# A retention and gated-MLP kernel: five reorderings, of block 1's scaling, of GpSimd's sums, of stores and transposes in SP's queue, and of the last tile's results

## The chip, the cores and the metric

The kernel runs on one core of a Trainium2 chip. A core has five engines with instruction streams of their own: TensorE (PE, matrix products into PSUM), VectorE (DVE), ScalarE (ACT), GpSimd (POOL) and SyncE (SP, which here only issues DMAs). They meet through semaphores. The metric is the device time of one execution in microseconds; lower is better. PSUM has eight banks; the kernel's tags `n` and `st` hold one bank each, `a`, `b` and `m` two each.

## The reference

Retention attention for 8 batches, 8 heads, 576 positions and head size 64, and behind it a layer of 512 to 2048 to 512 with the activation h cos(h), without a bias or a softmax:

```python
def _attn_ref(q, k, v):
    scale = 1.0 / np.sqrt(D_)
    scores = scale * np.matmul(q, k.transpose(0, 1, 3, 2))
    gamma = 1.0 - 2.0 ** (-5.0 - np.arange(H))
    rel = pos[:, None] - pos[None, :]
    Dmat = np.where(rel >= 0, gamma[:, None, None] ** rel[None, :, :], 0.0)
    return np.matmul(scores * Dmat, v)

def _moe_ref(x, w_in, w_out):          # x: 4608 x 512
    h = x @ w_in                       # 512 x 2048
    g = h * np.cos(h)
    return g @ w_out                   # 2048 x 512
```

Inputs and the output are float32.

## The kernel before

The 4608 tokens are cut into 18 **blocks** of 256 (`j`) and into 9 **tiles** of 512 (`n`, two blocks each).

*Retention.* gamma to the power of a difference is a product of a factor of the row and one of the column, so q and k are scaled by tables of powers (`scaled`, L167), rounded to bf16, transposed, and multiplied (`scores`); a mask leaves the causal half (`ret`, L262, L292). Within 128 tokens the sum over v is direct (`out_own`, L375); everything earlier comes through a running state (`sums_of`, L319, with the adds at L338 to L349), whose rounded copy multiplies q (`out_carried`, L407). The sum of both is copied as `xT`.

*Transposes.* Blocks 0 to 3 are transposed on TensorE (`transpose_pe`, L210, with a copy at L215). Blocks 4 to 17 are transposed by DMA (`transpose_dma`, L197), 14 in all, issued on SP. `step` prepares one block: q and k scaled on GpSimd (`prep`), the DMA transpose, v rounded on GpSimd, and then the loads of a later block (`load`, five to eight DMAs on SP). So GpSimd's and SP's queues hold the blocks in the order in which the program calls `step`, together with the stores of results (`stored_rows`, L579). Below, "transpose 8" is that of block 8.

*The layer.* `mm1` makes h in PSUM for four or two rows of 128 of the 2048, ScalarE takes the cosine (as a sine of h plus pi/2, L457) and VectorE multiplies (L460) into `gT`. The second product of tile 0 is direct (L927). From tile 1 on it is done as seven products instead of eight on 2x2 blocks (`mm2_seven`, `product`, L563), with sums of quarters of `gT` (`g_sum`, L503, called `gs`) and of the weights (`w_sums`, L483) ahead of them. Product x has the numbers 1 to 7; the order is 1, 2, 4, 6, 5, 7, 3 in tile 1 and 1, 2, 6, 4, 7, 5, 3 later. Results are copied from PSUM by ScalarE (`copied`, L593), added up by VectorE (L589), and stored as four quarters c11, c21, c22 and u1 (store numbers 0, 1, 2 and 3). Adds and stores are put on a list `pend` and run at the next `flush`. After a store of a given number, `stored` may call `steps_to`, which prepares blocks up to a number.

*Sums on GpSimd.* VectorE makes most of the `gs`; GpSimd makes that of product 3 in tile 1 and that of product 7 later, in pieces of 128x512. In tile 1 the work of `first_scores` lies between products 4 and 6: the second halves of gs 5 and gs 6, the mask products of block 4, gs 3, gs 7 and the state sums of block 5.

*The last tile.* Its product 5 is computed in three pieces, one of 256 columns and two of 128, and product 3 is accumulated on the same pieces, so that the last adds and stores are small. In `product` the first piece has the tag `b`; the two small ones share a tile with the tag `m`. Stores alternate between SP and ScalarE for c22 and for the last three pieces.

The order of the instructions on each engine is that of the program: the schedule is written by hand, and only waits on semaphores are put in by the framework. It tracks them by tile: a reader of a tile waits for its last writer. `after` adds a wait by hand, for which `g_sum` has the argument `gate`.

Of the kernel before, what the change touches and what calls it, by code (L numbers as in the profile page):

```python
# [8 lines left out]
F32 = mybir.dt.float32  # L9
# [8 lines left out]
def kernel(  # L18
# [9 lines left out]
    nc = tc.nc  # L28
    P = 128
# [12 lines left out]
    E2 = ET // 2  # L42
# [489 lines left out]
    def product(n, x, halfway=None):  # L532
        gT = tiles["g", n]
        parts = [(j, 0, N2) for j in range(2)]
        fold = n in (1, last)
        fresh = x not in ((6, 7, 3) if fold else (6, 7))
        if fresh:
            tag = {1: "n", 2: "st", 4: "m" if n == 1 else "st", 5: "st", 3: "n"}[x]
            if x == 5 and n == last:
                ps = psum.tile([P, N2], F32, tag="b", name="o")  # L540
                pt = psum.tile([P, 2, 512], F32, tag="m", name="o")
                tiles["o", x] = [ps] + [pt[:, k, : N2 // 2] for k in range(2)]
            else:
                ps = psum.tile([P, 2, N2], F32, tag=tag, name="o")
                tiles["o", x] = [ps[:, j] for j in range(2)]
                tiles["all", x] = ps
        if x in (5, 3) and n == last:
            parts = [(0, 0, N2), (1, 0, N2 // 2), (1, N2 // 2, N2)]
        dst = tiles["o", x if fresh else 5 if x == 3 else 1]
        lhs = {1: gT[:, :E2, :256], 2: gT[:, E2:, :256], 4: gT[:, E2:, 256:]}.get(x)  # L550
        if lhs is None:
            lhs = tiles["gs", n, x]
        rhs = {1: w_quarter(0, 0), 2: w_quarter(1, 0), 3: w_quarter(1, 1)}.get(x)
        if rhs is None:
            rhs = w_sum[x]
        order = [(e, i) for e in range(E2) for i in range(len(parts))]
        if len(parts) > 2:
            order.sort(key=lambda u: u[1])
        for u, (e, i) in enumerate(order):
            if halfway and u == len(order) // 2:  # L560
                halfway()
            j, c0, c1 = parts[i]
            nc.tensor.matmul(  # L563
                dst[i],
                lhsT=lhs[:, e, j * P : (j + 1) * P],
                rhs=rhs[:, e, c0:c1],
                start=(fresh and e == 0 and (i == 0 or len(parts) > 2)),
                stop=(e == E2 - 1 and (i == len(parts) - 1 or len(parts) > 2)),
                skip_group_check=True,
            )  # L570
        return parts
# [9 lines left out]
    def mm2_seven(n, at, stored, xs=(1, 2, 6, 4, 7, 5, 3), halfway=None):  # L581
# [13 lines left out]

        def store(t, r, c, s):
            def go():
                queues = (nc.sync, nc.scalar) if n == last and s == 2 else (nc.sync, nc.sync)
                stored_rows(n * W + r * 256, c * N2, (c + 1) * N2, t, queues)
                stored(s)  # L600

            return go

        for x in xs:
            if x in at:
                at[x](flush, pend)
            else:
                flush()
            if x == 6 and n > 1:
                late_sums(n, (3,))  # L610
            parts = product(n, x, halfway)
            if x == 1:
                c11 = copied("a", 1)
                tiles["c11"] = c11
                if n > 1 and 2 not in at:
                    late_sums(n, (5, 6))
            elif x == 2:
                c11 = tiles["c11"]
                if n == 1:
                    p2 = copied("d", 2)  # L620
                    continue
                pend[:0] = [add(c11, c11, tiles["all", 2]), store(c11, 0, 0, 0)]
            elif x == 6:
                u1 = copied("b", 1)
            elif x == 4:
                c21 = copied("c", 4)
            elif x == 7 and n == 1:
                pend += [
                    add(c21, c21, tiles["all", 1]),
                    add(c22, c22, tiles["all", 1]),  # L630
                    store(c21, 1, 0, 1),
                    store(c22, 1, 1, 2),
                    add(c11, c11, p2),
                    store(c11, 0, 0, 0),
                ]
            elif x == 7:
                c22 = copied("d", 1)
                pend += [add(c21, c21, tiles["all", 1]), store(c21, 1, 0, 1)]
            elif x == 5 and n == 1:
                c22 = copied("d", 5)  # L640
            elif x == 5 and n == last:
                for (j, c0, c1), ps in zip(parts, tiles["o", 5]):
                    pend.append(add(c22[:, j, c0:c1], ps, c22[:, j, c0:c1]))
                pend.append(store(c22, 1, 1, 2))
            elif x == 5:
                pend += [
                    add(c22, c22, tiles["all", 5]),
                    add(u1, u1, tiles["all", 5]),
                    store(c22, 1, 1, 2),
                ]  # L650
            elif n < last:
                pend += [add(u1, u1, tiles["all", 5 if n == 1 else 3]), store(u1, 0, 1, 3)]
                flush()
            else:
                flush()
                for (j, c0, c1), ps in zip(parts, tiles["o", 5]):
                    add(u1[:, j, c0:c1], ps, u1[:, j, c0:c1])()
                    stored_rows(
                        n * W + j * P, N2 + c0, N2 + c1, u1[:, j : j + 1, c0:c1],
                        (nc.sync, nc.scalar),  # L660
                    )
# [124 lines left out]
    load_next(names="kqv", gate=w_dma[3])  # L786
    ps0 = psum.tile([P, DG, BK], F32, tag="m", name="ov")
    out_own(0, ps0)
    transpose_pe(1, "k", "st", vec, (1,))
    scaled(nc.vector, 1, "q", 0)  # L790
    scaled(nc.vector, 1, "q", 1)
    out_carried(0, ps0)
    act(x_of(0), ps0)
    nc.scalar.activation(sine, half_pi, ACTF.Sin, bias=0.0, scale=1.0)
# [70 lines left out]
    for n in range(NT):  # L865
        blocks = blocks_of.get(n) or [(e + k * E2, 0, W) for e in range(0, E2, 2) for k in range(2)]
        for i, (et, c0, cw) in enumerate(blocks):
# [11 lines left out]
            if (n, i) == (1, 0):  # L879
                step(False)  # L880
                load_next()
                for r0, ot in stores:
                    stored_rows(r0, 0, DM, ot)
            if (n, i) == (1, 1):
                step(False)
                load_next()
                step()
            if (n, i) == (1, 3):
# [75 lines left out]

        def first_scores(flush, pend):
            g_sum(n, 5, 4, E2)
            g_sum(n, 6, 4, E2)
            masks = scores(a, "ab")
            add_a = sums_of(a, "st")
            add_b = sums_of(b, "m")  # L970
            masks[0]()
            add_a()()
            masks[1]()
            g_sum(n, 3, 0, E2)
            g_sum(n, 7, 0, 4)
            tiles["rounded"] = add_b()
            g_sum(n, 7, 4, E2)

        def next_scores(flush, pend):
            outputs(a, "a")  # L980
# [30 lines left out]

        def stored(u):
            if n == 1:
                steps_to({2: 8}.get(u, 0))
            else:
                steps_to({0: 2 * n + 6, 3: 2 * n + 7}.get(u, 0))

# [31 lines left out]
```

## Time and profile before

| | before |
|---|---|
| median of 3 runs | 296.59 us (295.59 to 298.37) |
| the profiled execution | 296.28 us |
| its span, first to last instruction | 294.6 us |
| TensorE busy | 283.2 us (96%) |
| VectorE busy | 215.6 us (73%) |
| ScalarE, GpSimd busy | 143.0, 145.6 us (49% each) |
| mean granted TensorE clock | 0.994 |
| data moved by DMA | 49.78 MB |
| median from issue to landing: store of 128 KB, transpose | 2.6, 5.1 us |

Times in a view count from the start of the span. In the chain that ended last a row has its start, its length and what it is: an engine with the tile and the line, or a DMA from issue to landing. In the timeline a row has start, length, engine, line, operation, what is written from what, shapes and a count; rows of the same kind that follow each other are merged, and behind them stands how long the engine had been idle and what ended that. `SPq` and `ACTq` are the queues of SP and ScalarE in which DMAs are issued: the length there is that of the issue, not of the transfer. In the list of waits a row has who waited for whom, the total, how often, and the longest.

### The profile page before, as it was taken

The numbers are of one execution on the slowest core, as the hardware profiler recorded it, in microseconds if no ns is written. First come the engines' busy times: TensorE is split into PE (matmuls) and PEld (weight loads), VectorE is DVE, ScalarE is ACT, GpSimd is POOL, SyncE is SP. The second block draws the span as 40 slices with busy tenths as digits, with TensorE's granted clock in tenths as the row PEclk, the third lists the DMA queues.
The fourth block names the chain that finished last, engine by engine and source line by source line (L and its number), as shares of the span: only waits on it lengthen the run. The fifth ranks groups of instructions, "written<-read, shape, count | busy, mean of one in ns | idle before, by whom it ended". The sixth has DMA issues, their size and how long they took to land.

```text
span 294.6 us, 7623 instructions
## 1 busy us (share of the span) xinstructions
PE 283.2 (96%) x3248; PEld 195.0 (66%) x3268; DVE 215.6 (73%) x268; ACT 143.0 (49%) x166; POOL 145.6 (49%) x172
## 2 busy tenths in 40 slices
PE   7889999999999999999999999999999999999993
PEld 2568755878864688458845884588458845874583
DVE  4585748558986999699659965996599659835933
ACT  4466537646436624563356335633563356326620
POOL 8641535847864495839713961497148014102400
PEclk9799999999999999999999999999999999999999
DMA  7999999999899999999999999979930630121014
GB/s 197 268 222 215 232 247 214 231 181 231 198 199 227 204 240 210 191 219 197 236 203 193 243 215 197 219 128 223 203 64 21 127 71 0 38 65 44 2 37 107
DMA packets 128930, 49.78 MB, mean 169 GB/s; under 512 B 89344, under 2 KB 128384, under 8 KB 128896
## 3 DMA queue, kind: packets, MB, share of 16 engines
q1 hardware_dynamic: 124288, 44.84, 75.6%
q0 software_dynamic: 4224, 4.19, 8.8%
q8 instruction: 25, 0.41, 0.6%
q10 hardware_dynamic: 384, 0.26, 0.4%
q14 instruction: 9, 0.07, 0.1%
HBM read 36.70 MB, written 9.44 MB: 157 GB/s over the span
## 4 chain that ended last, share of the span: by engine, by line
PE 79%; DVE 10%; DMA 4%; POOL 2%; ACT 2%; issue 1%; DVEq 0%; ACTq 0%
PE h L445 38%; PE o L563 27%; PE o L927 5%; DVE gT L460 3%; PE ov L375 3%; DVE gs L503 3%; DMA qkT<-qks 2%; PE st L319 2%; POOL qks L167 2%; PE sc L282 2%; DVE ret L292 2%; PE ov L407 1%; DMA fk<-in_k_dram 1%; PE tr L210 1%; ACT cosh L457 1%
## 5 line engine op out<-in xcount | busy, mean ns | idle before, releaser
L445 PE MATMUL h<-xT,w_in_sb 128*128 128x512 bf16 (+1 forms) x690 | 126.6, 340 | 1.0
L460 DVE TENSOR_TENSOR gT<-h,cosh 128x1024 bf16<-128x1024 f32 x72 | 87.9, 1221 | 37.5 <-ACT cosh L457 37.4
L457 ACT ACTIVATE cosh<-h,half_pi 128x1024 f32<-128x1024 f32 x72 | 80.2, 1114 | 66.4 <-PE h L445 65.1
L445 PEld LDWEIGHTS <-w_in_sb 128*128 128x128 bf16 x704 | 68.4, 98 | 55.3 <-issue 0.6
L503 POOL TENSOR_TENSOR gs<-gT 128x512 bf16<-128x512 bf16 x28 | 35.8, 1280 | 92.2 <-DVE gT L460 92.2
L563 PEld LDWEIGHTS <-gs 128*128 128x128 bf16 x528 | 49.5, 98 | 6.4
L167 POOL TENSOR_TENSOR qks<-fq,gq 128x512 bf16<-128x512 f32 x31 | 33.9, 1113 | 18.1 <-DMA fq<-in_q_dram 14.9
L563 PEld LDWEIGHTS <-gT 128*128 128x128 bf16 x384 | 37.1, 98 | 6.3
L593 ACT COPY ot<-o 128x512 f32<-128x512 f32 x33 | 19.3, 586 | 40.5 <-PE o L563 40.5
L167 POOL TENSOR_TENSOR qks<-fk,gkc 128x512 bf16<-128x512 f32 x28 | 31.8, 1154 | 0.0
L589 DVE TENSOR_TENSOR ot<-ot,o 128x512 f32<-128x512 f32 x35 | 23.2, 680 | 10.9 <-ACT ot L593 7.9
L563 PE MATMUL o<-w_out_sb,gs 128*128 128x256 bf16 (+1 forms) x264 | 30.6, 269 | 0.0
L563 PE MATMUL o<-ws,gs 128*128 128x256 bf16 (+1 forms) x264 | 30.5, 270 | 0.0
L563 PE MATMUL o<-w_out_sb,gT 128*128 128x256 bf16 x256 | 30.5, 273 | 0.0
L292 DVE TENSOR_TENSOR ret<-sc,mask_c 128x1024 bf16<-128x1024 f32 x25 | 29.7, 1214 | 0.1
L430 ACT CAST xT<-ov 128x1024 bf16<-128x1024 f32 x16 | 16.2, 1013 | 11.0 <-PE ov L407 11.0
L178 POOL CAST vb<-fv 128x512 bf16<-128x512 f32 x31 | 18.7, 624 | 5.7 <-DMA fv<-in_v_dram 5.6
L503 DVE TENSOR_TENSOR gs<-gs,gT 128x1024 bf16<-128x1024 bf16 x16 | 15.7, 982 | 0.3
L503 DVE TENSOR_TENSOR gs<-gT 128x512 bf16<-128x512 bf16 (+1 forms) x25 | 15.4, 615 | 0.4
L563 PE MATMUL o<-ws,gT 128*128 128x256 bf16 x128 | 15.3, 273 | 0.0
L349 DVE TENSOR_TENSOR s<-st,s 128x256 f32<-128x256 f32 x18 | 7.6, 421 | 10.4 <-PE st L319 10.1
L359 ACT CAST sb<-s 128x512 bf16<-128x512 f32 (+1 forms) x18 | 10.3, 573 | 9.3 <-DVE s L347 3.8
(81 smaller groups left out, 203.4 us busy)
## 6 DMA issues: line engine op xcount, KB each, us to landing
out_dram<-ot SPq DMA_DIRECT2D x69, 128.0 KB, 2.6
fk<-in_k_dram SPq DMA_DIRECT2D x25, 256.0 KB, 5.7
fv<-in_v_dram SPq DMA_DIRECT2D x25, 256.0 KB, 5.1
fq<-in_q_dram SPq DMA_DIRECT2D x12, 512.0 KB, 5.3
w_in_sb<-in_moe_w_in_dram POOLq DMA_DIRECT2D x4, 512.0 KB, 8.1
w_out_sb<-in_moe_w_out_dram POOLq DMA_DIRECT2D x4, 512.0 KB, 9.8
fk<-in_k_dram SPq DMA_DIRECT2D x3, 512.0 KB, 5.3
fv<-in_v_dram SPq DMA_DIRECT2D x3, 512.0 KB, 7.0
```

The source lines that it names most:

```text
L167: return eng.tensor_tensor(out=dst.rearrange("p b a d -> p a b d"), in0=src.rearrange("p (a b) d -> p a b d", a=2), in1=by.rearrange("p (a ...
L178: runs[y](vb[:, y], f[:, :, y, :] if j < NP_B else f[:, y])
L292: nc.vector.tensor_tensor(out=ret[:, k].rearrange("p a b i -> p (a b) i"), in0=pss[k].rearrange("p a b i -> p (a b) i"), in1=mask.unsqueez ...
L430: evac(x, ps)
L445: nc.tensor.matmul(ps[:, j, :], lhsT=w_in_sb[:, dg, (et + j) * P : (et + j + 1) * P], rhs=xT[:, dg, c0 : c0 + w], start=(dg == 0), stop=(d ...
L457: nc.scalar.activation(cosh, ps, ACTF.Sin, bias=half_pi, scale=1.0)
L460: nc.vector.tensor_mul(gT[:, et : et + m, c0 : c0 + w], ps, cosh)
L503: i = eng.tensor_tensor(out=tiles["gs", n, x][:, e : e + step], in0=a[:, e : e + step], in1=b[:, e : e + step], op=op_,)
L563: nc.tensor.matmul(dst[i], lhsT=lhs[:, e, j * P : (j + 1) * P], rhs=rhs[:, e, c0:c1], start=(fresh and e == 0 and (i == 0 or len(parts) > 2)),
L589: return lambda: nc.vector.tensor_tensor(out=out_, in0=in0, in1=in1, op=ALU.add)
L593: nc.scalar.copy(t, tiles["all", x])
L927: nc.tensor.matmul(pss[t], lhsT=gT[:, e, t * P : (t + 1) * P], rhs=w_out_sb[:, e, :], start=(e == 0), stop=(e == ET - 1),)
```

## The change

- Block 1's two scalings of q on VectorE stand ahead of the transpose and copy of the second half of its k.
- The stores of tile 0 stand behind the preparation of block 5 and no longer ahead of it, the fourth row first. The steps that tile 1's third store (c22) set off are set off by its fourth (u1).
- In tile 1, GpSimd's sum for product 3 is cut in two halves. The first waits for VectorE's second half of gs 6, the other for its second half of gs 7.
- In the last tile, the add and store of c21 are called at once behind product 7 and ahead of the copy of c22; of the store of c21 one half is issued on ScalarE, as that of c22 was already.
- In the last tile, the two small pieces of products 5 and 3 have a PSUM tile of their own each, with the tags `m` and `a`.

No instruction is added or taken away on an engine; one DMA moves from SP's queue to ScalarE's.

```diff
--- before.py
+++ after.py
@@ -537,9 +537,10 @@
         if fresh:
             tag = {1: "n", 2: "st", 4: "m" if n == 1 else "st", 5: "st", 3: "n"}[x]
             if x == 5 and n == last:
-                ps = psum.tile([P, N2], F32, tag="b", name="o")
-                pt = psum.tile([P, 2, 512], F32, tag="m", name="o")
-                tiles["o", x] = [ps] + [pt[:, k, : N2 // 2] for k in range(2)]
+                tiles["o", x] = [
+                    psum.tile([P, c], F32, tag=t, name="o")
+                    for t, c in (("b", N2), ("m", N2 // 2), ("a", N2 // 2))
+                ]
             else:
                 ps = psum.tile([P, 2, N2], F32, tag=tag, name="o")
                 tiles["o", x] = [ps[:, j] for j in range(2)]
@@ -595,7 +596,7 @@
 
         def store(t, r, c, s):
             def go():
-                queues = (nc.sync, nc.scalar) if n == last and s == 2 else (nc.sync, nc.sync)
+                queues = (nc.sync, nc.scalar) if n == last and s else (nc.sync, nc.sync)
                 stored_rows(n * W + r * 256, c * N2, (c + 1) * N2, t, queues)
                 stored(s)
 
@@ -634,8 +635,10 @@
                     store(c11, 0, 0, 0),
                 ]
             elif x == 7:
+                pend += [add(c21, c21, tiles["all", 1]), store(c21, 1, 0, 1)]
+                if n == last:
+                    flush()
                 c22 = copied("d", 1)
-                pend += [add(c21, c21, tiles["all", 1]), store(c21, 1, 0, 1)]
             elif x == 5 and n == 1:
                 c22 = copied("d", 5)
             elif x == 5 and n == last:
@@ -786,9 +789,9 @@
     load_next(names="kqv", gate=w_dma[3])
     ps0 = psum.tile([P, DG, BK], F32, tag="m", name="ov")
     out_own(0, ps0)
-    transpose_pe(1, "k", "st", vec, (1,))
     scaled(nc.vector, 1, "q", 0)
     scaled(nc.vector, 1, "q", 1)
+    transpose_pe(1, "k", "st", vec, (1,))
     out_carried(0, ps0)
     act(x_of(0), ps0)
     nc.scalar.activation(sine, half_pi, ACTF.Sin, bias=0.0, scale=1.0)
@@ -879,10 +882,10 @@
             if (n, i) == (1, 0):
                 step(False)
                 load_next()
-                for r0, ot in stores:
-                    stored_rows(r0, 0, DM, ot)
             if (n, i) == (1, 1):
                 step(False)
+                for r0, ot in stores[3:] + stores[:3]:
+                    stored_rows(r0, 0, DM, ot)
                 load_next()
                 step()
             if (n, i) == (1, 3):
@@ -964,17 +967,18 @@
 
         def first_scores(flush, pend):
             g_sum(n, 5, 4, E2)
-            g_sum(n, 6, 4, E2)
+            six = g_sum(n, 6, 4, E2)
             masks = scores(a, "ab")
             add_a = sums_of(a, "st")
             add_b = sums_of(b, "m")
             masks[0]()
             add_a()()
             masks[1]()
-            g_sum(n, 3, 0, E2)
+            g_sum(n, 3, 0, 4, gate=six)
             g_sum(n, 7, 0, 4)
             tiles["rounded"] = add_b()
-            g_sum(n, 7, 4, E2)
+            seven = g_sum(n, 7, 4, E2)
+            g_sum(n, 3, 4, E2, gate=seven)
 
         def next_scores(flush, pend):
             outputs(a, "a")
@@ -1011,7 +1015,7 @@
 
         def stored(u):
             if n == 1:
-                steps_to({2: 8}.get(u, 0))
+                steps_to({3: 8}.get(u, 0))
             else:
                 steps_to({0: 2 * n + 6, 3: 2 * n + 7}.get(u, 0))
 
```

## The prediction

> **What bounds the kernel now.** I read the chain that ended last first, in order of time, because the change touches five separate places and only the chain says which of them sets the end.
>
> ```profile
> PE 79%; DVE 10%; DMA 4%; POOL 2%; ACT 2%; issue 1%; DVEq 0%; ACTq 0%
> ```
>
> ```profile
> 14.49 0.43 DVE qkT L215
> 14.91 1.21 DVE qks L167 x2
> ...
> 108.92 6.22 DMA qkT<-qks
> 115.14 0.04 issue
> 115.19 0.64 PE sc L282 x32
> ...
> 277.65 12.41 PE o L563 x128
> 290.08 0.29 DVE ot L589
> ```
>
> TensorE is busy 283.2 of 294.6 us. Before 18 us the chain runs through VectorE; at 115.19 us scores wait for a DMA transpose; after that it is TensorE without a break up to the last product. So a gain ahead of 115 us counts only if that transpose lets it through, and every wait added behind it counts in full. Next the waits of TensorE: all that exceeds 0.3 us, once the start is left out, is small.
>
> ```profile
> PE tr L210 <- DVE qks L167: 2.2, 6, 0.7
> PE sc L282 <- DVE s L349: 0.4, 1, 0.4
> PE ov L375 <- DVE ret L292: 0.2, 1, 0.2
> PE sc L282 <- DMA qkT<-qks: 0.2, 1, 0.2
> ```
>
> **Part 1, block 1's q scaled ahead of the copy.** In the timeline of VectorE the copy at 14.49 us waits 1.37 us for transposes, while q's scaling (14.83, 1.28 us for two) needs only q of block 1, which landed at 12.2 (issued 4.97, 7.3 to landing). After the change scaling runs at 13.12 to 14.41 and hides in that wait; the copy of k stays at 14.49. TensorE's transposes of q, now at 15.57 and 16.17, can follow its two idle matmuls at 15.0, so the two copies run at 15.45 and 15.87 and end at 16.3 instead of 17.02. Scores of block 1 start at 16.35, not 17.08: **-0.75 us**. Cover behind it: the next matmuls need weights that landed at 14.5, 19.9 and 22.4 us (issue plus 7.2, 7.2, 9.0); the tightest, at about 23.4 now and 22.65 then, keeps 0.3 us.
>
> **Part 2, GpSimd's sums in halves.** The timeline of VectorE in the second tile's products:
>
> ```profile
> 75.16 1.53 DVE L503 TENSOR_TENSOR gs<-gs,gT 128x1024 bf16<-128x1024 bf16 x1
> 76.61 2.34 DVE L292 TENSOR_TENSOR ret<-sc,mask_c 128x1024 bf16<-128x1024 f32 x2
> 78.88 1.60 DVE L503 TENSOR_TENSOR gs<-gT 128x1024 bf16<-128x1024 bf16 x1
> 80.40 0.87 DVE L349 TENSOR_TENSOR s<-st,s 128x256 f32<-128x256 f32 x2
> 81.19 0.68 DVE L503 TENSOR_TENSOR gs<-gT 128x1024 bf16<-128x1024 bf16 x1
> ```
>
> The same 128x1024 sum takes 0.68 us alone and 1.53 and 1.60 us while GpSimd's four sums run (74.50 to 79.94). The gates put GpSimd's first two behind the first of these and its last two behind the last, so VectorE saves 0.85 + 0.92 = 1.77 us. GpSimd's first half then takes two of its undisturbed 1.15 us and ends about when the second sum begins; its last half runs some 80.5 to 82.8, ahead of product 3 at 84.9 and of its own next work at 83.83, which waits for a load. So nothing queued behind the gated sums is late. TensorE gets back its two waits here, 0.38 us for s and 0.25 us for ret: **-0.63 us**. The Trainium skill (SBUF — State Buffer, Who interferes with whom) says that the second to start fully blocks until the first is done; the 1.60 us row agrees, since GpSimd's last sum ended at 79.93 and 0.68 more gives 80.6 against 80.48. By that rule a GpSimd half that ran late would cost one sum up to 1.15 us again, which changes nothing in the total below.
>
> **Part 3, order on SP's queue.** Two moves. Transpose 5 goes ahead of the first tile's eight stores: it is issued at about 68.9 us instead of 74.88, and its scores come at 80.55 where it now lands at 79.4, so it leaves the way free for the earlier TensorE. The eight stores move some 3 us back; the first reuse of their buffers waits for the store that is put first. The other move is that all eight stores of the second tile go ahead of transpose 7, four of them formerly behind the loads of block 9:
>
> ```profile
> 93.85 3.14 SPq L579 DMA_DIRECT2D out_dram<-ot  x4
> 97.59 2.27 SPq L197 DMA_TRANSPOSE qkT<-qks  x1
> 99.90 0.72 SPq L135 DMA_DIRECT2D fq<-in_q_dram  x1
> ...
> 105.25 3.56 SPq L579 DMA_DIRECT2D out_dram<-ot  x4
> 108.92 3.10 SPq L197 DMA_TRANSPOSE qkT<-qks  x1
> ```
>
> SP issues back to back from 38 to 130 us, so its order is the order of landing, and TensorE's pace doesn't reach it. Transpose 7 is issued 3.1 to 3.6 us later, lands at 104 to 106, and is needed at 111: free. Transpose 8, the one TensorE waits for, has the same work ahead of it: 97.03 + 3.14 to 3.56 for four stores + 7.66 (from transpose 7 to the end of five loads) = 107.8 to 108.3, up to 1.2 more if transpose 5 behind loads holds SP 3.3 to 3.6 us like its likes instead of 2.27. GpSimd has its input by 107.4 now, earlier then. But it stands right behind loads now. The two that stand so take 6.9 and 6.7 us to landing (issues 58.20, 84.42); the shortest of any takes 4.4, this one 6.2. That gives 112.2 at best, 114.5 to 116.4 with the likes of it; I take **115.3**. TensorE, 1.38 us earlier, would be there at 113.6 (114.97 less 1.38). It waits, and starts at 115.35 instead of 115.19: parts 1 to 3 together **+0.15 us**; between -1.6 (no wait at all: 1.38 and the present 0.22) and +3.1 (below).
>
> **Part 4, the last tile.** The end is a chain of four engines:
>
> ```profile
> 286.42 0.59 ACT L593 COPY ot<-o 128x512 f32<-128x512 f32 x1 [1.16 <-PE o L563]
> ```
>
> ```profile
> 287.04 0.69 DVE L589 TENSOR_TENSOR ot<-ot,o 128x512 f32<-128x512 f32 x1 [4.51 <-ACT ot L593]
> 287.65 1.03 DVE L589 TENSOR_TENSOR ot<-o,ot 128x256 f32<-128x256 f32 x3
> ```
>
> ```profile
> 288.76 0.73 ACTq L579 DMA_DIRECT2D out_dram<-ot  x1
> ```
>
> ScalarE copies c22, VectorE adds c21, then the three pieces of c22; product 3 at 288.12 follows the first piece's add. The change turns it round: the add of c21 starts at 286.42 and ends at 287.11; ScalarE's queue then holds a store that waits for this add, and only behind it the copy. An issue on ScalarE took 0.47 to 0.73 us, so the copy runs from about 287.85 to 288.45 instead of ending at 287.01. Queued behind the copy: VectorE's first c22 piece (288.45 instead of 287.65), behind that product 3 on TensorE, which waits for it, and the final adds. **+0.80 us**. Own results for the pieces let the add of the middle piece start 0.4 us sooner, and moving a store off SP frees 0.60 us of SP; but SP's last three stores (289.79, 290.58, 291.22) follow each other at issue pace from the first piece's add (ends 289.61), which is itself 0.8 later. They gain 0.1 at most: SP was free at 289.70. The Trainium skill (DMA: Bandwidth & Descriptors, Issuing engines are not separate DMA queues) says that a second issuing engine saves only issue time, usually small beside the transfer; 0.60 against 2.4 us to landing agrees. By that the move to ScalarE buys at most its 0.60 on SP, nothing in landing.
>
> **Sum.** The profiled execution took 296.28 us (span 294.6), 0.31 under the median of 296.59. 296.28 + 0.15 + 0.80 = **297.2 us**, 0.2% over the median. A measurement of this kernel tells about 1% (3 us) from no change.
>
> **Rivals.**
> *Transpose 8 lands early.* With stores filling the gaps that transposes leave, loads come sooner and it lands by 113.6. For: 4.4 us is the shortest latency. Against: both transposes behind loads took 6.7 or more. 296.28 - 1.6 + 0.8 = 295.5.
> *Slower: the late transpose 7 is not made good.* In the rows eight stores keep SP for 6.7 us while each needs about 0.35 us of transfer (so far apart land those queued behind loads); if the DMA engines stand idle meanwhile, transpose 7 and the loads behind it slip by 3.1 us, and transpose 8 with them, to 118.2: 296.28 + 3.1 + 0.8 = 300.2. It passes 1% once 2.2 of the 3.1 are lost. Against: four stores fewer behind the loads give 3.56 back.
> *ScalarE is not held by its issue.* Then the copy starts at 287.2, and the tail costs 0.15: 296.6.
> *The gates do not part the two engines* (rows of 1.5 us stay): -0.63 goes, but transpose 8 decides all the same: 297.2.
>
> **Chances.** Forecast (the last rival in it) 0.50, early transpose 0.20, cheap tail 0.15, slower 0.11; 0.04 for a gain of over 1%, for which the profile has no source: removable waits add to 1.6 us. Runs of one kernel scatter (up to 298.37 before), which puts 0.01 of the forecast over the bound: faster 0.04, same 0.84, slower 0.12. The range leaves out the far half of the slow rival and the quickest of the early one: 295.3 to 299.3.
>
> **What would show it.** Right: scores of block 1 at 16.4; gs sums of 0.7 us near 75 and 78; TensorE waiting 1 to 2 us for a transpose near 114; ScalarE's copy of c22 ending near or after 2 us behind product 7, and product 3 waiting 0.8 us for VectorE. Wrong: no wait near 114 (then the DMA order gained), or a wait of over 3 us there; a last copy as soon as now.

## The result, and the profile after

The changed kernel took **299.84 us** (median of six runs, 299.56 to 302.02), the kernel before 296.22 in the same measurement (295.59 to 298.37). The ratio is 1.0127, with a 95% interval of 1.0082 to 1.0171. The prediction of 297.2 us, in a range of 295.3 to 299.3, was too low: the change makes the kernel slower by 1.3%, and not by 0.2%.

The profiled execution of the changed kernel took 299.81 us, with a span of 298.1 us against 294.6 before. The views of this section are of this pair. In the changed file the lines behind the edited store function stand one further down, so that L563, L579, L589 and L593 of before are L564, L580, L590 and L594 here.

The first view is the chain that ended last, in order of time (start, length, what). This is the piece of it that answers to the transpose at 108.92 us and the scores at 115.19 before:

```profile
109.82 6.32 DMA qkT<-qks
116.14 0.04 issue
116.18 1.01 PE sc L282 x32
117.20 3.09 PE o L564 x16
```

Transpose 8 is issued 0.9 us later and lands 1.00 us later than before. That is not all: the scores behind it take 1.01 us instead of 0.64, and the product behind them 3.09 us, where the same sixteen matmuls took 1.85 (3.16 and 1.92 us in the timeline, which counts each to its end). The waits of TensorE (what waited for what: us in total, times, longest) say how long it stood:

```profile
PE sc L282 <- DMA qkT<-qks: 3.2, 1, 3.2
...
PE o L564 <- DVE ot L590: 1.0, 1, 1.0
```

The waits of 0.38 us for s and 0.25 us for ret are gone, as forecast. Two others have come. The first was 0.22 us and is 3.19; the second, near the end, did not exist. The table by stretches of time explains the long matmuls. Its columns are the stretch, its length, the busy time of TensorE (with the number of instructions), the granted clock, the share of the DMA engines (a packet counts in the stretch in which it starts, so this can pass 1) and GB/s. These two stretches of the changed kernel follow each other:

```profile
112.88:116.29 3.41, 0.22 (x18) 1.00 0.78 147
116.29:119.71 3.42, 3.42 (x45) 0.50 1.20 264
```

After a stretch of 3.41 us in which TensorE worked for 0.22 us, its clock was 0.50 for the next 3.41 us. In the kernel before, the granted clock is 1.00 all through these microseconds.

The fourth tile's first h product (`n` = 3; one of the expectations below calls it the third tile) starts at 120.13 us, where it started at 117.52. From there to the last tile the two kernels run in step, since the last h product starts at 266.28 against 263.68. The last landing follows it by 30.43 us, against 29.61. So the time lost can be written down in three terms:

| where | before | after | difference |
|---|---|---|---|
| landing of transpose 8 | 115.14 | 116.14 | +1.00 |
| from that landing to the fourth tile's first h | 2.38 | 3.99 | +1.61 |
| from the last tile's first h to the last landing | 29.61 | 30.43 | +0.82 |
| sum (the span grew by 3.5) | | | +3.43 |

The first line holds for this pair alone. Two kernels below differ from the one before only in the last tile, and their transpose 8 landed at 114.25 and 113.75 us. The landing scatters by over a microsecond from execution to execution, so one pair of profiles doesn't say what moved it.

The tail shows in the timeline (start, length, engine, line, operation; in brackets the idle time before it, and what ended that):

```profile
287.28 0.59 ACT L594 COPY ot<-o 128x512 f32<-128x512 f32 x1 [1.16 <-PE o L564]
...
289.08 0.69 DVE L590 TENSOR_TENSOR ot<-ot,o 128x512 f32<-128x512 f32 x1 [3.95 <-issue]
...
289.80 0.74 ACTq L580 DMA_DIRECT2D out_dram<-ot  x1
290.66 0.59 ACT L594 COPY ot<-o 128x512 f32<-128x512 f32 x1 [2.79 <-PE o L564]
291.28 0.82 DVE L590 TENSOR_TENSOR ot<-o,ot 128x256 f32<-128x256 f32 x3 [1.51 <-ACT ot L594]
291.76 1.93 PE L564 MATMUL o<-w_out_sb,gs 128*128 128x256 bf16 x24 [1.00 <-DVE ot L590]
```

The order is the one the prediction drew. The add of c21 comes first; ScalarE's queue holds a store for it until 290.54; only then does the copy of c22 run, at 290.66. VectorE's first add of c22 waits for the copy, and product 3 waits 1.00 us for that add.

Lastly, SP's queue around transposes 5 and 6, where the change put transpose 5 ahead of the first tile's stores. First the kernel before, then the changed one:

```profile
68.96 5.81 SPq L579 DMA_DIRECT2D out_dram<-ot  x8
74.88 2.27 SPq L197 DMA_TRANSPOSE qkT<-qks  x1
...
84.42 3.26 SPq L197 DMA_TRANSPOSE qkT<-qks  x1
```

```profile
68.46 4.41 SPq L197 DMA_TRANSPOSE qkT<-qks  x1
72.97 5.04 SPq L580 DMA_DIRECT2D out_dram<-ot  x8
...
84.32 4.43 SPq L197 DMA_TRANSPOSE qkT<-qks  x1
```

Transpose 5 now holds SP for 4.41 us instead of 2.27, and transpose 6, which was not moved, for 4.43 instead of 3.26.

### The profile page after: what moved, and what is told of

Read it like the earlier page. It is cut to its first block, busy times and chain, and to the rows that moved or that the text cites. A ratio compares the mean times of both kernels' runs of the same rounds, so it can differ in the third digit from the quotient of the medians.

```text
span 298.1 us, 7627 instructions
## 1 busy us (share of the span) xinstructions
PE 284.2 (95%) x3248; PEld 195.3 (66%) x3268; DVE 215.1 (72%) x268; ACT 143.0 (48%) x166; POOL 144.3 (48%) x172
## 4 chain that ended last, share of the span: by engine, by line
PE 79%; DMA 9%; DVE 3%; POOL 2%; ACT 1%; issue 1%; SPq 1%; ACTq 0%; POOLq 0%
PE h L445 37%; PE o L564 29%; PE o L930 5%; DMA w_in_sb<-in_moe_w_in_dram 3%; PE ov L375 3%; DMA fk<-in_k_dram 2%; DMA qkT<-qks 2%; PE sc L282 2%; DVE gT L460 2%; DMA fq<-in_q_dram 2%; PE st L319 2%; POOL qks L167 2%; PE ov L407 1%; SPq L135 1%; ACT cosh L457 1%
## 5 line engine op out<-in xcount | busy, mean ns | idle before, releaser
L564 PEld LDWEIGHTS <-gs 128*128 128x128 bf16 x528 | 50.1, 99 | 8.2 <-issue 1.3
L564 PEld LDWEIGHTS <-gT 128*128 128x128 bf16 x384 | 37.1, 98 | 6.3
L594 ACT COPY ot<-o 128x512 f32<-128x512 f32 x33 | 19.3, 586 | 42.1 <-PE o L564 42.1
L564 PE MATMUL o<-w_out_sb,gs 128*128 128x256 bf16 (+1 forms) x264 | 31.8, 276 | 1.0 <-DVE ot L590 1.0
L590 DVE TENSOR_TENSOR ot<-ot,o 128x512 f32<-128x512 f32 x35 | 23.2, 681 | 12.0 <-issue 4.2
L564 PE MATMUL o<-ws,gs 128*128 128x256 bf16 (+1 forms) x264 | 30.5, 270 | 0.0
L564 PE MATMUL o<-w_out_sb,gT 128*128 128x256 bf16 x256 | 30.5, 273 | 0.0
L564 PE MATMUL o<-ws,gT 128*128 128x256 bf16 x128 | 15.3, 273 | 0.0
```

The source lines that it names most:

```text
L564: nc.tensor.matmul(dst[i], lhsT=lhs[:, e, j * P : (j + 1) * P], rhs=rhs[:, e, c0:c1], start=(fresh and e == 0 and (i == 0 or len(parts) > 2)),
L590: return lambda: nc.vector.tensor_tensor(out=out_, in0=in0, in1=in1, op=ALU.add)
L594: nc.scalar.copy(t, tiles["all", x])
```

## The experiments

There were three questions. What do parts 1 and 2 (scaling ahead of the copy, GpSimd's halves) bring on their own? Which edit makes transpose 8 late? How much of the loss is the clock? The first theory was that the late transpose follows from the steps being moved to the fourth store, that the tail costs what was forecast, and that the clock falls because TensorE stands still for 3.2 us. Each kernel was run several times beside the kernel before on the same chip.

**The gains alone.** Parts 1 and 2 are put into the kernel before, and nothing else.

```diff
-    transpose_pe(1, "k", "st", vec, (1,))
     scaled(nc.vector, 1, "q", 0)
     scaled(nc.vector, 1, "q", 1)
+    transpose_pe(1, "k", "st", vec, (1,))
...
-            g_sum(n, 6, 4, E2)
+            six = g_sum(n, 6, 4, E2)
...
-            g_sum(n, 3, 0, E2)
+            g_sum(n, 3, 0, 4, gate=six)
             g_sum(n, 7, 0, 4)
             tiles["rounded"] = add_b()
-            g_sum(n, 7, 4, E2)
+            seven = g_sum(n, 7, 4, E2)
+            g_sum(n, 3, 4, E2, gate=seven)
```

> The kernel before with only block 1's q scaled ahead and GpSimd's sums in halves. Theory (transpose 8 sets when block 8's scores start): it lands near 115.1 us as before, TensorE arrives 1.4 to 2 us earlier and waits 1.5 to 2.3 us for it, the end doesn't move: 0 us, within 0.5. If such a wait already halves the clock, +1.6. Rival (TensorE's own pace sets the time): -1.4 us.

It took 296.17 us against 296.55 for the kernel before, a ratio of 1.0000 (0.9977 to 1.0024). In the timeline of TensorE the gains are there; block 8's scores show where they end:

```profile
16.42 0.64 PE L244 MATMUL sc<-qkT 64*64 64x128 bf16 x32 [0.19 <-DVE qkT L215]
```

```profile
114.86 0.64 PE L282 MATMUL sc<-qkT 64*64 64x128 bf16 x32 [1.10 <-DMA qkT<-qks]
```

Scores of block 1 start at 16.42 us instead of 17.08. TensorE is done with block 7's work at 113.77 instead of 114.97. Then it waits 1.10 us for transpose 8, which lands at 114.82. A gain of 1.2 us ahead of this transpose is worth 0.3 behind it (h of the fourth tile at 117.19 instead of 117.52).

**The steps alone.** Only the second tile's steps move to its fourth store, so that all its stores go ahead of transpose 7.

```diff
-                steps_to({2: 8}.get(u, 0))
+                steps_to({3: 8}.get(u, 0))
```

> The kernel before with only one edit: the steps set off by the fourth store of tile 1 instead of the third, so all eight stores go ahead of transpose 7 and transpose 8 stands right behind loads. Theory (its place in the queue costs): it lands near 116.1 instead of 115.1 us, TensorE waits 1.2 us, +1.0 us and no fall of the clock. Rival (the loss needs the other edits, this place is free): transpose 8 at 115.1 and 0 us.

It took 296.69 us, a ratio of 1.0006 (0.9988 to 1.0023). Transpose 8 was issued at 108.41 and landed at 115.39, only 0.25 us later than before. The expected 1 us did not come (the interval ends at +0.7 us), so this edit by itself is not the cause, and the first theory falls.

**The tail alone.** Results of their own for the last pieces, half of c21's store on ScalarE (both edits are shown with the copy-first kernel below), and the add of c21 ahead of the copy of c22.

```diff
+                pend += [add(c21, c21, tiles["all", 1]), store(c21, 1, 0, 1)]
+                if n == last:
+                    flush()
                 c22 = copied("d", 1)
-                pend += [add(c21, c21, tiles["all", 1]), store(c21, 1, 0, 1)]
```

> The kernel before with only the last tile's edits. Theory (ScalarE's store holds the copy of c22, and product 3 waits for the add behind it): the copy ends 2.2 us behind product 7 instead of 0.6, product 3 waits 1.0 us for VectorE, +0.9 to 1.0 us. Rival (the pieces' own results and the store taken off SP pay for it): -0.2 to 0.

It took 296.75 us, a ratio of 1.0008 (0.9989 to 1.0027). From the last tile's first h to the last landing it needs 30.46 us against 29.61, which is 0.85 more, and product 3 waits 1.00 us. The profile confirms the cost; the ratio does not resolve it. In this execution transpose 8 happened to land at 114.25, ahead of TensorE, which covers part of the loss.

**Idle matmuls in the wait.** The changed kernel with twelve matmuls on zeros ahead of block 8's scores. They keep TensorE at work while it waits, and their results are used for nothing.

```diff
+        if j == 8:
+            warm(12, sc_banks[0])
```

> The changed kernel with 12 idle matmuls on zeros ahead of block 8's scores, in the bank that these use; nothing else is moved. Theory (the wait of 3.2 us halves TensorE's clock for the next 3.4 us, which costs 1.6): the granted clock stays at 1.0 from 116 to 120 us, product 3 of tile 2 takes 1.9 instead of 3.1 us, -1.6 us against the changed kernel, about 298.2. Rival (that stretch is slow from DMA traffic or another engine): no change, 299.8.

It took 298.70 us, a ratio of 1.0066 (1.0044 to 1.0087).

```profile
113.30 2.76 PE L220 MATMUL idle<-zeros 128*128 128x512 bf16 x11
116.70 0.64 PE L282 MATMUL sc<-qkT 64*64 64x128 bf16 x32 [0.64 <-DMA qkT<-qks]
117.28 1.92 PE L564 MATMUL o<-w_out_sb,gs 128*128 128x256 bf16 x16
```

One of the twelve is missing from the records. The transpose lands even later here, at 116.66, but the scores take 0.64 us again and the product 1.92 (3.16 in the timeline of the changed kernel). From the landing to h it is 2.37 us, as in the kernel before (2.38), instead of 3.99. So the term of 1.61 us is the clock, and it goes away if TensorE is kept at work. The medians show 1.14 us of it, since the transpose was 0.5 us later. For every execution the mean granted clock is on record: it lies between 0.988 and 0.994 in the six of the changed kernel, and between 0.997 and 1.000 in the six of this one. (One step of 3.41 us at half clock lowers the mean by 0.006; the mean doesn't tell where the step lay.)

What remained was the later landing. It did not come from the steps alone, so the next runs took up the other move on SP's queue.

**Transpose 5 alone.** It goes ahead of the first tile's eight stores in the kernel before.

```diff
                 load_next()
-                for r0, ot in stores:
-                    stored_rows(r0, 0, DM, ot)
             if (n, i) == (1, 1):
                 step(False)
+                for r0, ot in stores[3:] + stores[:3]:
+                    stored_rows(r0, 0, DM, ot)
                 load_next()
```

> The kernel before with transpose 5 ahead of the first tile's stores, and nothing else of the change. Theory A (a transpose directly behind loads holds SP 4.4 us instead of 2.27, and the next one 4.4 instead of 3.3): transpose 8 is issued near 109.5 to 110 instead of 108.9 and lands near 115.8 to 116.2, so TensorE waits 0.9 to 1.2 us for it, no fall of the clock, 296.5 + 0.7 = 297.2. Rival B (the lateness needs both moves, or TensorE's earlier arrival): transpose 8 within 0.5 us of 115.1, 296.5.

It took 299.23 us against 296.34, a ratio of 1.0104 (1.0071 to 1.0138). One moved transpose, with none of the change's other edits, gives most of its loss.

```profile
68.89 4.18 SPq L197 DMA_TRANSPOSE qkT<-qks  x1
...
84.79 4.27 SPq L197 DMA_TRANSPOSE qkT<-qks  x1
...
111.52 3.11 SPq L197 DMA_TRANSPOSE qkT<-qks  x1
```

```profile
113.64:117.05 3.41, 1.10 (x55) 1.00 0.77 159
117.05:120.46 3.41, 3.41 (x21) 0.50 1.26 271
```

Transposes 5 and 6 hold SP nearly as long as in the changed kernel (4.18 and 4.27 us). Transpose 8 is issued 2.6 us later than before and lands at 116.40. TensorE waits 2.31 us, and the second block, the table by stretches for TensorE, shows that this is enough for the clock to fall. The expectation had the longer holds right. But the issue came 1.5 us later than it said, the wait was twice as long, and it had no fall of the clock. One of the four executions was faster, 297.85 us, and its mean clock was 1.000; the other three took 299.1 to 300.1 us at 0.989 to 0.994.

**Both moves.** Transpose 5 ahead of the stores and the steps on the fourth store; the other parts are left out.

```diff
-                for r0, ot in stores:
-                    stored_rows(r0, 0, DM, ot)
             if (n, i) == (1, 1):
                 step(False)
+                for r0, ot in stores[3:] + stores[:3]:
+                    stored_rows(r0, 0, DM, ot)
...
-                steps_to({2: 8}.get(u, 0))
+                steps_to({3: 8}.get(u, 0))
```

> The kernel before with both moves on SP's queue (transpose 5 ahead of the first tile's stores, steps on the fourth store of the second tile), TensorE's gains and the tail left as before. Theory A (the order of the queue alone makes transpose 8 late): issued near 109.8, lands 116.1 to 116.7; TensorE, there at 114.97, waits 1.2 to 1.7 us, too short for the clock to fall; 296.5 + 1.2 = 297.7. Rival B (it takes the earlier TensorE or the GpSimd halves): transpose 8 near 115.2 and 296.6. Rival C (a wait of this length already halves the clock): granted clock 0.5 behind it, 299.

It took 297.43 us, a ratio of 1.0055 (1.0029 to 1.0081). Transpose 8 was issued at 110.10 and landed at 116.09, as theory A had it, and TensorE was there at 114.18, without parts 1 and 2. The order of the queue is enough to make it late. But the wait of 1.96 us brought the clock down in the profiled execution, where A expected it to hold:

```profile
113.77:117.18 3.41, 1.45 (x56) 1.00 0.92 220
117.18:120.59 3.41, 3.19 (x16) 0.50 1.32 251
```

Of its twelve times, eight lie between 296.5 and 297.8 us and four between 298.8 and 299.3. The gap fits the clock's 1.6 us, and so does the mean granted clock: 0.994 to 1.000 in the eight, 0.990 to 0.994 in the four. So the fall happens in some executions of this kernel and probably not in the others; where in the execution it lies is seen only in the one with a profile.

**The copy first.** Results of their own for the pieces and half of c21's store on ScalarE, but the copy of c22 stays ahead of that store.

```diff
-                ps = psum.tile([P, N2], F32, tag="b", name="o")
-                pt = psum.tile([P, 2, 512], F32, tag="m", name="o")
-                tiles["o", x] = [ps] + [pt[:, k, : N2 // 2] for k in range(2)]
+                tiles["o", x] = [
+                    psum.tile([P, c], F32, tag=t, name="o")
+                    for t, c in (("b", N2), ("m", N2 // 2), ("a", N2 // 2))
+                ]
...
-                queues = (nc.sync, nc.scalar) if n == last and s == 2 else (nc.sync, nc.sync)
+                queues = (nc.sync, nc.scalar) if n == last and s else (nc.sync, nc.sync)
```

> The kernel before with results of their own for the last product's pieces and a store of c21 half on ScalarE, the copy of c22 left ahead of that store. Theory A (the late copy is the whole of the tail's cost): no wait of 1.0 us ahead of product 3, last start of h to last landing 29.3 to 29.6 instead of 30.46, 296.3. Rival B (the store on ScalarE delays the last pieces wherever it stands): 30.0 to 30.5, 296.8.

It took 296.07 us, a ratio of 1.0002 (0.9980 to 1.0023).

```profile
285.55 0.59 ACT L594 COPY ot<-o 128x512 f32<-128x512 f32 x1 [1.16 <-PE o L564]
286.17 0.69 DVE L590 TENSOR_TENSOR ot<-ot,o 128x512 f32<-128x512 f32 x1 [4.51 <-ACT ot L594]
...
287.24 1.93 PE L564 MATMUL o<-w_out_sb,gs 128*128 128x256 bf16 x24
```

Product 3 waits for nothing, and the tail takes 29.40 us instead of 29.61. So the store on ScalarE and the separate results are worth 0.2 us, too little to be measured in the whole time. The tail's loss is the place of the copy behind the store. All profiles agree: the tail takes 29.38 to 29.40 us in the three kernels with these edits and the copy first, 29.61 to 29.74 in the six with the tail of before, and 30.42 to 30.46 in the four with that of the change.

**Two stores held back.** Parts 1 and 2, the copy-first tail, and two of the second tile's stores (four issues on SP) kept back until transpose 8 has been issued.

```diff
+                if n == 1 and s in (0, 3):
+                    held.append((n * W + r * 256, c * N2, (c + 1) * N2, t))
+                    return
                 stored_rows(n * W + r * 256, c * N2, (c + 1) * N2, t, queues)
...
             if (n, i) == (2, 6):
-                step()
+                step(False)
+                for u in held:
+                    stored_rows(*u)
+                load_next()
```

> The kernel before with scaling ahead of the copy and GpSimd's halves (parts 1 and 2), two of the second tile's stores held back until transpose 8 and the loads around it are issued, and the tail of the copy-first kernel. Theory A (what TensorE gains by 85 us is lost only to the landing of transpose 8): transpose 8 is issued 3 to 3.5 us earlier, near 105.5, lands near 112, TensorE doesn't wait at 113, and the third tile's h starts near 115.9 instead of 117.5: 296.5 - 1.6 - 0.2 = 294.7. Rival B (a transpose behind loads lands near 115 whenever it is issued, or fq's landing holds its input): 296 to 296.5. Rival C (what is early there is lost at a later wait): transpose 8 near 112, yet 296.

It took **294.46 us**, a ratio of 0.9948 (0.9925 to 0.9972): faster than both kernels, by half a per cent against the one before.

```profile
103.33 1.08 SPq L149 DMA_DIRECT2D fv<-in_v_dram  x1
106.29 2.96 SPq L197 DMA_TRANSPOSE qkT<-qks  x1
109.34 2.65 SPq L580 DMA_DIRECT2D out_dram<-ot  x4
```

Transpose 8 is issued at 106.29 and lands at 111.25. TensorE doesn't wait, and the fourth tile's h starts at 116.07. What TensorE gained by 85 us now reaches the end. SP is free from 104.41 to 106.29, so its order no longer decides here: GpSimd's scaling of the transpose's input ends at 106.26. GpSimd does this work right behind its sums for the third tile's product 7, the last of which waited 1.93 us for VectorE's `gT`, so here the pace of the layer does reach the transposes; the prediction had said that TensorE's pace doesn't.

**Transpose 5 put back.** The changed kernel with all its edits except that transpose 5 stands behind the first tile's stores again.

```diff
                 load_next()
+                for r0, ot in stores:
+                    stored_rows(r0, 0, DM, ot)
             if (n, i) == (1, 1):
                 step(False)
-                for r0, ot in stores[3:] + stores[:3]:
-                    stored_rows(r0, 0, DM, ot)
                 load_next()
```

> The changed kernel with transpose 5 put back behind the first tile's stores; all else of the change stays. Theory A (that move is what makes transpose 8 late): transpose 8 is issued near 108.4 and lands near 115.3, as where only the steps were moved, so TensorE, there at 113.0, waits 2.3 us instead of 3.19. Of the 3.6 us that the change costs, 0.8 goes if the clock still falls in every run (299.0), 2.4 where a wait of 2.3 us no longer reaches it (297.4); the tail's 0.85 stays in both. Rival B (the steps' move alone holds transpose 8 back once TensorE is early): 116.1, wait 3.1, 299.8.

It took 297.73 us against 296.31, a ratio of 1.0060 (1.0039 to 1.0081).

```profile
115.30 0.64 PE L282 MATMUL sc<-qkT 64*64 64x128 bf16 x32 [1.78 <-DMA qkT<-qks]
115.87 1.92 PE L564 MATMUL o<-w_out_sb,gs 128*128 128x256 bf16 x16
```

```profile
111.59:115.00 3.41, 1.93 (x48) 1.00 0.86 194
115.00:118.41 3.41, 3.11 (x52) 1.00 1.30 259
```

Transpose 8 lands at 115.25, as theory A had it, 0.9 us earlier than in the changed kernel, and the clock holds. TensorE waits 1.78 us, parted between two stretches (1.48 and 0.30). In the other executions it does not always hold: two of the six took 298.39 and 299.03 us at mean clocks of 0.992 and 0.985, the other four 297.1 to 297.9 at 0.998 to 1.000. About half of the loss is gone with this one edit. What is left in the profiled execution, of 297.29 us, is the tail: h of the fourth tile starts at 117.63, only 0.11 later than before.

**The held stores without the holding.** Parts 1 and 2 and the copy-first tail. The edit is shown against the kernel with the held stores.

```diff
-                if n == 1 and s in (0, 3):
-                    held.append((n * W + r * 256, c * N2, (c + 1) * N2, t))
-                    return
...
-                step(False)
-                for u in held:
-                    stored_rows(*u)
-                load_next()
+                step()
```

> The held-stores kernel without the holding: the kernel before, parts 1 and 2, and the copy-first tail. Theory A (the held stores are what lets the gain through): transpose 8 lands near 114.8 again, TensorE waits about 1 us for it, 296.17 - 0.27 = 295.9. Rival B (parts 1 and 2 with the cheaper tail do it alone): 294.5.

It took 295.67 us, a ratio of 0.9987 (0.9960 to 1.0015), near the 295.9 of theory A. Transpose 8 lands at 114.59 and TensorE waits 1.53 us for it; h of the fourth tile starts at 116.96, against 116.07 with the stores held. The clock holds here too, and this table belongs with those above:

```profile
111.88:115.29 3.41, 1.88 (x74) 1.00 1.25 167
115.29:118.70 3.41, 3.41 (x25) 1.00 1.34 234
```

**Transpose 5 in the middle.** In the kernel before it stands behind four of the first tile's eight issues of stores, with four behind it.

```diff
-                for r0, ot in stores:
+                for r0, ot in stores[:2]:
                     stored_rows(r0, 0, DM, ot)
             if (n, i) == (1, 1):
                 step(False)
+                for r0, ot in stores[2:]:
+                    stored_rows(r0, 0, DM, ot)
```

> The kernel before with transpose 5 in the middle of the first tile's eight stores, four ahead of it and four behind. Theory A (a transpose holds SP until all that is ahead of it on the queue has landed): issued near 71.6, SP held until the fourth store's landing near 75.2, so 3.6 us, landing 2 us later at 77.2. Rival B (it holds SP some 2.2 us behind a store and 4.4 behind loads): SP free at 73.8, landing near 76.1. The time is near that of the kernel before in A (296.5 to 297.5), since SP is let go about when it was.

It took 296.39 us, a ratio of 1.0003 (0.9985 to 1.0020). Transpose 5 was issued at 72.36, held SP for 2.38 us, until 74.74, and landed at 77.15. The last store ahead of it landed at 74.83. Theory A, that SP is held until all ahead has landed, gives this to 0.1 us from the measured landing; B's 2.2 us fits too, since the issue itself came late. This run alone does not part them, but the traces of all kernels do. Each of the 78 transposes between 55 and 125 us was set beside the last landing that the trace has ahead of it on SP's queue. It lets SP go between 0.5 us before that landing and 0.9 us after it in all of them but four, which do so 1.1 to 1.7 us after it. Three of these were issued only 1.4 us ahead of that landing and kept SP for 2.4 to 2.8 us all the same, so a landing that is near does not seem to shorten the hold much below 2 us (the shortest of these 78 is 1.79 us; transpose 16, later on, is held for 1.6 to 1.7 in every kernel and let go 0.3 to 0.9 us ahead of the landing); with the fourth, a landing is missing from the records. Behind loads that land late the hold is 4.2 to 4.8 us (transpose 5 in the changed kernel: let go at 72.87, last load landed at 73.17; transpose 8: 114.17 and 114.27). Behind stores, each of which lands some 2.5 us after its issue, it is mostly 2.0 to 2.5 us. In this kernel the length of a transpose on SP's queue is thus, to within a microsecond, not its own: it goes with the time that the transfers ahead of it still need. No run changes that time and nothing else, so this is read from the traces and not shown by an edit.

## Why the prediction was wrong

**Part 1 was right.** It said -0.75 us and block 1's scores at 16.35. The gains alone put them at 16.42. In the changed kernel they come at 15.54, because its profiled execution lacks a stretch of half clock from 8.47 to 11.89 us that the one of before has. That is chance and not the change: six kernels that start exactly like the kernel before lack it too. Their scores come at 16.26 to 16.37, and at 15.46 to 15.57 in the five kernels that have part 1 and lack it, so part 1 is worth some 0.8 us.

**Part 2 was right on TensorE; its sums were taken too short.** Both waits went, as said. The rows of the two sums are these, in the timeline of the changed kernel, with the rows of GpSimd that ran beside them:

```profile
73.97 0.96 POOL L184 CAST v_odd<-fv 64x512 bf16<-64x512 f32 x1
74.49 0.98 DVE L503 TENSOR_TENSOR gs<-gs,gT 128x1024 bf16<-128x1024 bf16 x1
75.62 2.28 POOL L503 TENSOR_TENSOR gs<-gT,gs 128x512 bf16<-128x512 bf16 x2 [0.69 <-DVE gs L503]
77.66 0.79 DVE L503 TENSOR_TENSOR gs<-gT 128x1024 bf16<-128x1024 bf16 x1
```

GpSimd's sums are parted from the first of VectorE's, but the two sums take 0.98 and 0.79 us, not 0.68: VectorE saves 1.36 us instead of 1.77. The first still ran for 0.44 us beside GpSimd's cast of v (L184), which the prediction had not counted, and the second for 0.24 us beside the end of GpSimd's first half. Parts 1 and 2 together let TensorE be early by 1.20 us in the gains alone, where 1.38 was forecast.

**Part 3 failed in two steps.** The first is "I take 115.3" for the landing of transpose 8; it was 116.14, inside the 114.5 to 116.4 that the same sentence gave. Two terms ahead of it were too small.

- *The holds.* The working said that transpose 5 behind loads might hold SP up to 1.2 us longer. But with the 6.7 to 6.9 us from issue to landing, 115.3 stands for an issue at 108.4 to 108.6, so most of that was left out. Transpose 5 held SP 2.14 us longer (4.41 against 2.27). The eight stores now followed it, so the next loads went out 0.87 us later (78.06 instead of 77.19) and landed later (the last ahead of transpose 6 at 88.89 instead of 87.68), and transpose 6 held SP 1.17 us longer. The second tile's stores started 0.69 us later for that, and transpose 7 was issued at 100.98, where the sum gives 100.2 to 100.6.
- *The loads behind transpose 7.* The sum took 7.66 us from its issue to the end of the five loads. Here it was 8.84:

```profile
94.54 6.27 SPq L580 DMA_DIRECT2D out_dram<-ot  x8
100.98 2.09 SPq L197 DMA_TRANSPOSE qkT<-qks  x1
...
109.82 4.35 SPq L197 DMA_TRANSPOSE qkT<-qks  x1
```

With the steps alone it was 8.41 and with transpose 5 put back 9.04, so this term doesn't come from transpose 5. From the issue of transpose 7 to that of transpose 8 the kernel before took 11.33 us, and 11.80 to 12.36 in five other kernels that keep transpose 5 behind stores and four stores in between. The one profile from which the 7.66 was read had it shorter than all of these.

Transpose 8 was therefore issued at 109.82 and not at 107.8 to 108.3. From issue to landing it took 6.32 us, within the forecast's 6.2 to 6.9. That transpose 5's move is what makes it late against the kernel before is seen in all profiles: with transpose 5 behind the first tile's stores, or in the middle of them, transpose 8 landed at 113.75 to 115.39 us (eight kernels, without the one with held stores), and with it ahead of them at 116.09 to 116.66 (four kernels).

The second failed step is what was made of the wait. The prediction counted it as its length and looked no further: TensorE at 113.6, landing at 115.3, **+0.15 us** in all. The wait was longer at both ends (113.00 to 116.18; that TensorE was there earlier than forecast is the chance told under part 1, for the gains alone had 113.77), and it carried a cost that stood in no term of the sum, the 1.61 us of half clock. The runs with idle matmuls and with transpose 5 put back show that this term goes when the wait is filled and, in most executions, when it is shorter.

The rival that ends on the slower side gave 300.2 us, near what was measured, but it is not what happened. It had transpose 8 at 118.2 because eight stores in a row leave the DMA engines idle; the steps alone, which have those eight stores, show transpose 8 at 115.39 and no loss that can be measured. That the total came near this rival's is luck.

**Part 4 was right.** +0.80 us was forecast; the tail grew by 0.82 in the changed kernel and by 0.85 on its own, by the mechanism described, and leaving the copy first makes it 0.2 us shorter than before.

The sum, against the profiled executions: 296.28 + 0.95 was forecast. Adding 0.84 for transpose 8 and 1.61 for the clock gives 299.68, where 299.81 was measured.

**What stays open.** Transpose 8 was issued at 111.52 us with transpose 5 alone and at 110.10 with both moves, so moving the steps gives back part of what the other move costs; why the loads between transposes 7 and 8 vary by over a microsecond from kernel to kernel, and why transpose 8 needs 4.9 to 7.0 us from issue to landing, is not explained by any row. And a transpose between 55 and 125 us lands 1.5 to 4.2 us after it has let SP go, which the hold does not explain either.

## What to carry to other kernels

Before moving a transfer forward on a queue, look at what will then stand directly ahead of it: here a DMA transpose kept its queue until about the time when everything ahead had landed, so ahead of the stores it waited out the loads, and the stores that used to fill this time had to stand in line. A wait of TensorE is not always worth its length: one of some 2 us, within 3.4 us of time, may cost 1.6 us more in clock, so a forecast with a wait of that size needs a second term, or work to keep TensorE busy. And a gain ahead of a fixed landing is worth nothing until that landing comes earlier too; taking two stores out of the transpose's way brought 1.2 us by the medians (295.67 to 294.46, with intervals that overlap a little, 0.9960 to 1.0015 and 0.9925 to 0.9972), where the gain itself had brought nothing that could be measured.

## What the runs showed of the hardware that was not expected

The granted clock fell after waits far shorter than expected. In every trace, what the record gives for it changes only at steps of 3.41 us, and each step goes by how busy TensorE was in the step before: 0.22, 1.10 and 1.45 us of work in 3.41 were followed by a clock of 0.50, and 1.88 and 1.93 us by 1.00 (the five tables above). In the gains alone, 1.57 us in a step near the end was followed by 1.00, so the limit would lie between 43% and 46% of a step. A wait of 1.96 us that falls into one step can thus cost 1.6 us, and a wait of 1.53 us in one step, or one of 1.78 us that is parted between two steps, nothing. In the first 12 us this limit is not sharp: 56 to 58% of a step was followed by 0.50 in two kernels and by 1.00 in three others.

The Trainium skill (TensorE: Matmul & The Clock Gate, What's actually happening) says that the clock is decided in free-running windows of 3413 ns, and that half clock comes after at least one idle window. The steps of 3.41 us agree with the first. The second is too generous as a rule for this kernel: in none of the three steps was TensorE idle throughout, and waits of 3.19, 2.31 and 1.96 us were enough. Where the Trainium skill (TensorE: Matmul & The Clock Gate, HAM oscillation — how this bites in real kernels) sums it up as no idle gaps over about 3.4 us, these runs say that about 2 us can be too long.
